# The order of a 27,000-instruction program is chosen among several hundred plans, and the first chunk's y gets tiles of its own

## Chip, core and metric

One core of a Trainium2 chip. The metric is the device time of one execution in microseconds, the median of several runs. The kernel is timed on one core; nothing is shared with the others.

## The reference

An RWKV-7 attention block, then a feed-forward block with SiLU. Everything is float32 on the chip.

```python
# r, k, v, w, a, b: (batch 4, heads 8, seq 768, head_dim 40)
for t in range(S):
    y[:, :, t] = np.einsum('bhd,bhde->bhe', rt, state)
    Sa = np.einsum('bhde,bhe->bhd', state, at)
    state_decay = state * wt[:, :, None, :] - np.einsum('bhd,bhe->bhde', Sa, bt)
    state = state_decay + np.einsum('bhd,bhe->bhde', vt, kt)
...
x = y.transpose(0, 2, 1, 3).reshape(3072, 320)
h = x @ w_in                      # (320, 2048)
g = h * (1.0 / (1.0 + np.exp(-h)))
out = g @ w_out                   # (2048, 320)
```

w_in and w_out come in as float64 and are turned into float32 on the chip.

## The kernel before

The sequence is cut into 12 chunks of 64 steps. Within a chunk the recurrence is solved in closed form: products of decays by scans on VectorE (DVE), products of a with b and k (`between`), the inverse of a unit triangular 64x64 matrix for each of the 32 pairs of batch and head, then u = X R (`solve`, `solve_t`), y from u, v and the state (`look`, `write`, `write_state`, `scaled`), and the new state (`update`). Each chunk's y, 256 tokens by 320, goes through the feed-forward block (`moe`): `full` and `rest` are x @ w_in, `gate` is Silu on ScalarE, `second` (L1319) is g @ w_out.

The functions, with the lines where their instructions are recorded:

- `load` (L449, L459) and `load_r` (L476, L485): inputs of a chunk, on SP's DMA queue. `prepare(n)`: scans (`down` L509 to L511, `between_`, `up` L529), kb (`aside` L548) and a (`scale` L538) on DVE, `between` (L566), `masked` (L613), `sv` (L628), R's copy (L640), `turn` (L653) and its copies to kt (L666).
- `special(n)`, chunks 0 to 2: the inverse from 16-blocks. The blocks go through memory (ms L583, xs L755), `dots` on DVE (L679, L680), back through zs (L765) to mi (L771), then `both` (L797), `turn` (L810) and three `more` (L842), each with an addition on DVE (L857).
- `inverse(k)` and `merge(n)`, chunks 3 to 11: two chunks at a time, 32-blocks by `dots` on DVE, out through zd (L879) and, after a copy on ScalarE (L885), xd (L886), and back (L897, L909); `merge` joins halves with two TensorE operations, `first` (L923) and `second` (L952).
- `chain(n)`: `right` (L995), `total` (L1005), `solve` (L1019), `solve_t` (L1050), a transpose of the state (L1080, copy L1093), `update` (L1107) and two additions to the state (L1123).
- `read(n)`: two `look` (L1149), masked on DVE (L1161), `write_state` (L1185), `write` (L1200), `scaled` (L1211). Chunk 0 does `write` and `scaled` in two halves and sends y straight to the x tile `xt` by twelve transfers, six on SP and six on ScalarE (L1254); the others send it through memory (L1229, then `bring`, L1269, L1271).
- `moe(n)`: `full` (L1281), `rest` (L1294), `gate` (L1304), `second` (L1321), copy (L1333), output (L1336).
- `weights(n)`: ten pieces of the weights, each 1 MB as float64, fetched by GpSimd (L363) into space that is otherwise used later (the g tile, parts of wo, a raw tile, the XI tile), and converted by DVE and ScalarE (L368 to L386); three pieces use TensorE for a sum (`sum_`, L392).

All of these only record operations. `Plan.add` notes engine, estimated cost, what is read and written, a priority `pri`, and the `Room`s that the operation needs: a room is one of four PSUM tile pairs (`pair`) or one of two SBUF tiles (`lam`), which it holds until its last operation. `Plan.order` (L100) makes one list of all operations: at each step it takes, for every engine, the ready operation with the least estimated start plus `URGE[engine] * pri`, and of these the earliest. For TensorE the estimate counts instruction blocks and half speed before 42 us (`walk`). The list is emitted as it is, so each engine works through its own part in that order, and a semaphore wait at its head holds back all that is behind it. What goes to SP's, ScalarE's and GpSimd's DMA queues stands in the same list.

In `read(0)` the two `look` results and y take `lam` rooms, of which there are two; chunk 1's `masked` takes the same kind:

```python
pl, la = Room("pair", 2), Room("lam", 3)
...
py_, yx = {part: Room("pair", 3 if n else 2) for part in parts}, Room("lam", 1)
```

Of the kernel before, what the change touches and what calls it, by code (L numbers as in the profile page):

```python
# [3 lines left out]

# [26 lines left out]


class Plan:

# [65 lines left out]
    def order(self):  # L100
        ops = self.ops
        self.fetched, self.count, self.shape = [0.0, 0.0], 0, "Q"
        nexts = [[] for _ in ops]
        for op in ops:
            op["wait"] = len(op["before"])
            for b in op["before"]:
                nexts[b].append(op)
        ready = {e: [op for op in ops if op["engine"] == e and not op["wait"]] for e in self.HOP}
        at = dict.fromkeys(self.HOP, 0.0)
        out, held = [], {}  # L110
        queue = dict.fromkeys(("SP", "ACT", "POOL"), 0.0)
        for op in ops:
            op["ready"] = 0.0
        while len(out) < len(ops):
            best = None
            for e, some in ready.items():
                starts = []
                for op in some:
                    s = max(at[e], op["ready"])
                    for room in op["rooms"]:  # L120
                        if room.slot is None:
                            free = self.free[room.kind]
                            fits = free and held.get((room.kind, room.most), 0) < room.most
# [45 lines left out]
            out.append(op)  # L169
        return out  # L170

@with_exitstack
def kernel(
    ctx: ExitStack,
# [17 lines left out]
    D, H, P, Q = 40, 8, 4, 16  # L192
# [35 lines left out]
    at = ring("a", 3, Q * C)  # L228
# [29 lines left out]
    def vec(n):  # L258
        return 0.15 + n * 0.00104
# [871 lines left out]
    def read(n):  # L1131
# [7 lines left out]
        lam = []  # L1139
        for m in range(2):  # L1140
            pl, la = Room("pair", 2), Room("lam", 3)
# [14 lines left out]

            add("PE", 0.9, look, rk + vtk + [("ut", m)], [pl], pri, [pl, la], 128)
            add(
                "DVE",
                vec(1024),  # L1160
                lambda pl=pl, la=la: nc.vector.tensor_tensor(  # L1161
                    out=la.tile.rearrange("p (q t) -> p q t", q=Q),
                    in0=pl.tile.rearrange("p a b -> p (a b)").rearrange("p (q t) -> p q t", q=Q),
                    in1=ml.unsqueeze(1).to_broadcast([128, Q, C]),
                    op=ALU.mult,
                ),
                [pl],
                [la],
                pri,
                [pl, la],  # L1170
            )
# [46 lines left out]
        for part in parts:  # L1218
            used = [lam[m] for m in part]
            if n:  # L1220
                add("PE", 0.9, partial(write_state, py_[part]), [*rk, "GT"], [py_[part]], pri, [py_[part]], 128)
            add("PE", 0.87 * len(part), partial(write, part, py_[part]), ktk + used, [py_[part]], pri, [py_[part], *used], 64 * len(part), shape="H")
            add("DVE", vec(512 * len(part)), partial(scaled, part, py_[part]), [py_[part], *allw], [yx if len(part) == 2 else (yx, part)], pri, [py_[part], yx] if part is parts[0] else [py_[part]])
        yxk = [yx] if len(parts) == 1 else [(yx, part) for part in parts]
        if n >= ND:
            yx.left = 3
            for j in range(2):
                dma(
                    lambda j=j: nc.sync.dma_start(  # L1229
                        xh[n].rearrange("(p j e) t -> j e p t", p=P, j=2)[j],  # L1230
                        yx.tile[rows(j)].rearrange("e (p t) -> e p t", p=P),
                    ),
                    160,
                    yxk,
                    [("xh", n, j)],
                    pri,
                    rooms=[yx],
                )
            return
        pieces_ = []  # L1240
# [8 lines left out]
        for i, (h, r0, r1, d) in enumerate(pieces_):  # L1249
            k = r0 // 128  # L1250
            e = "ACT" if n == 0 and i % 2 else "SP"
            p0, s0 = d.start + r0 - 128 * k, 64 * (h % 2) + r0 - D * h
            dma(
                lambda h=h, k=k, e=e, p0=p0, s0=s0, m=r1 - r0: (nc.scalar if e == "ACT" else nc.sync).dma_start(  # L1254
                    xt[p0 : p0 + m, k], yx.tile[s0 : s0 + m, h // 2 * T : h // 2 * T + T]
                ),
                (r1 - r0) * 1.0,
                yxk,
                [("xt", k + (k == 2 and d.start > 0), h)],
                pri,  # L1260
                e,
                [yx],
            )

    def bring(n):
# [270 lines left out]
```

## Time and profile before

| | us |
|---|---|
| median of 3 runs | 747.25 |
| lowest, highest | 745.65, 751.07 |
| profiled execution, its own time | 744.45 |
| profiled execution, first to last instruction (span) | 742.7 |
| TensorE busy | 673.2 |
| VectorE busy | 418.7 |
| ScalarE busy | 193.7 |
| first TensorE matmul starts | 13.34 |
| first `full` of chunk 0 starts | 74.55 |
| first `full` of chunk 1 starts | 154.58 |
| last `second` ends | 735.0 |

Times in the profile count from the first instruction. PE is TensorE, PEld its weight loads, DVE VectorE, ACT ScalarE, POOL GpSimd, SPq and ACTq the queues by which SP and ScalarE issue transfers. A wait names the engine and the line that ended last before it; "issue" is time in which nothing that the profile records was missing. The slices on the page are 18.6 us each; a digit is a share in tenths. PEclk is the clock that TensorE was granted. A float32 matmul shows as two records, so an operation of 32 matmuls has x64.

### The profile page before, as it was taken

What the parts mean: (1) busy time and instruction counts of PE and PEld (TensorE: products, weight loads), DVE (VectorE), ACT (ScalarE), POOL (GpSimd) and SP (SyncE); (2) the same over time, 40 slices, a digit from 0 to 9 for tenths busy, and PEclk for the clock granted to TensorE, in tenths of its full rate; (3) what the DMA queues carried; (4) which work ended last, traced back from release to release, by engine and by line L of the source; (5) the groups of instructions that cost most, each with busy time, mean ns of one, the idle gap of its engine ahead of it and who ended that gap; (6) DMA issues with size and microseconds to landing.
All of it is one profiled execution on the core that took longest, in us unless ns stands there. A gap on an engine that the chain in (4) does not pass through costs nothing.

```text
span 742.7 us, 27297 instructions
## 1 busy us (share of the span) xinstructions
PE 673.2 (91%) x12666; PEld 541.9 (73%) x12666; DVE 418.7 (56%) x614; ACT 193.7 (26%) x241; POOL 16.8 (2%) x31
## 2 busy tenths in 40 slices
PE   2177989999899999999699999999998999999995
PEld 2175668678778788877578878878877778778774
DVE  6847679797479345388228595372694576111000
ACT  3252626423303313104211405222115112102020
POOL 3300000000000000000000000000000000000000
PEclk9999999899999999999899999999997999999999
DMA  7670665722731554514334706443315213201001
GB/s 246 157 224 25 185 211 172 212 67 59 173 98 54 122 145 120 155 25 98 80 95 125 200 9 153 109 124 101 92 36 113 82 38 94 62 16 41 18 1 22
DMA packets 117979, 77.15 MB, mean 104 GB/s; under 512 B 65506, under 2 KB 114338, under 8 KB 117218
## 3 DMA queue, kind: packets, MB, share of 16 engines
q1 hardware_dynamic: 113352, 64.54, 33.3%
q0 software_dynamic: 2096, 10.49, 4.3%
q8 instruction: 101, 1.65, 0.9%
q10 hardware_dynamic: 2410, 0.30, 0.3%
q14 instruction: 20, 0.16, 0.1%
HBM read 60.29 MB, written 14.61 MB: 101 GB/s over the span
## 4 chain that ended last, share of the span: by engine, by line
PE 77%; DVE 8%; issue 5%; DMA 3%; SPq 2%; ACT 2%; ACTq 0%; DVEq 0%
PE pair L1321 27%; PE pair L1281 19%; PE pair L1294 5%; PE pair L1149 3%; PE pair L1200 3%; PE pair L566 3%; PE pair L842 2%; PE pair L1107 2%; PE pair L1019 2%; PE pair L628 2%; PE pair L1050 2%; PE pair L392 2%; PE pair L952 2%; PE pair L995 1%; PE pair L1185 1%
## 5 line engine op out<-in xcount | busy, mean ns | idle before, releaser
L1321 PE MATMUL pair<-wo,gts 128*128 128x320 f32 x768 | 219.6, 442 | 1.5 <-issue 1.5
L1321 PEld LDWEIGHTS pair<-wo,gts 128*128 128x128 f32 x768 | 145.1, 193 | 60.8 <-issue 5.0
L1281 PE MATMUL pair<-xt,wi 128*128 128x256 f32 x768 | 177.9, 390 | 3.4 <-DMA xt<-lam 3.4
L1281 PEld LDWEIGHTS pair<-xt,wi 128*128 128x128 f32 x768 | 147.3, 195 | 26.6 <-issue 4.5
L1304 ACT ACTIVATE gts<-pair 128x1024 f32<-128x1024 f32 x48 | 46.5, 1020 | 120.4 <-PE pair L1294 113.2
L1333 DVE COPY ot<-pair 128x320 f32<-128x320 f32 x24 | 11.7, 488 | 88.2 <-PE pair L1321 87.1
L680 DVE TENSOR_REDUCE XI<-XI 128x64 f32<-128x512 f32 (+9 forms) x85 | 58.6, 690 | 2.9
L566 PE MATMUL pair<-a,kb 40*64 40x64 f32 x1536 | 31.4, 233 | 30.1 <-issue 16.0
L566 PEld LDWEIGHTS pair<-a,kb 40*64 40x64 f32 x1536 | 27.8, 145 | 32.6 <-issue 30.7
L1161 DVE TENSOR_TENSOR lam<-pair,ml 128x1024 f32<-128x1024 f32 x24 | 29.1, 1222 | 37.0 <-PE pair L1149 37.0
L1294 PE MATMUL pair<-xt,wi 64*128 64x256 f32 x384 | 48.0, 389 | 0.0
L1294 PEld LDWEIGHTS pair<-xt,wi 64*128 64x128 f32 x384 | 35.2, 187 | 6.3 <-issue 2.0
L1211 DVE TENSOR_TENSOR lam<-pair,wz 128x1024 f32<-128x1024 f32 (+1 forms) x13 | 14.8, 1142 | 38.5 <-PE pair L1200 38.4
L679 DVE TENSOR_TENSOR XI<-XI,mi 128x1024 f32<-128x1024 f32 (+8 forms) x60 | 33.6, 560 | 3.0 <-DMA mi<-md 1.6
L640 ACT COPY R<-pair 128x640 f32<-128x640 f32 x12 | 8.3, 692 | 98.4 <-PE pair L628 98.3
L548 DVE TENSOR_TENSOR kb<-kbv 128x512 f32<-128x512 f32 (+1 forms) x36 | 29.9, 859 | 0.4
L1149 PEld LDWEIGHTS pair<-r,vut 40*64 40x64 f32 x1536 | 24.8, 135 | 6.1 <-issue 4.5
L1149 PE MATMUL pair<-r,vut 40*64 40x64 f32 x1536 | 27.8, 221 | 0.4 <-issue 0.4
L511 DVE TENSOR_TENSOR_SCAN kbv<-wz,zt 128x1024 f32<-128x1024 f32 x12 | 27.5, 2291 | 0.6
L529 DVE TENSOR_TENSOR_SCAN wz<-wz,zt 128x1024 f32<-128x1024 f32 x12 | 27.5, 2290 | 0.3
L1200 PEld LDWEIGHTS pair<-lam,kt 128*40 128x40 f32 x768 | 22.1, 117 | 5.8 <-issue 3.3
L885 ACT COPY mi<-XI 128x1024 f32<-128x1024 f32 x5 | 10.1, 2015 | 62.3 <-DVE XI L680 62.3
(144 smaller groups left out, 690.7 us busy)
## 6 DMA issues: line engine op xcount, KB each, us to landing
wz<-in_wT SPq DMA_DIRECT2D x12, 512.0 KB
kbv<-in_bT SPq DMA_DIRECT2D x12, 512.0 KB
a<-in_aT SPq DMA_DIRECT2D x12, 512.0 KB
kbv<-in_kT SPq DMA_DIRECT2D x12, 512.0 KB
r<-in_rT SPq DMA_DIRECT2D x48, 96.0 KB
vut<-in_vT SPq DMA_DIRECT2D x48, 96.0 KB
vu<-in_v SPq DMA_DIRECT2D x24, 160.0 KB
out<-ot SPq DMA_DIRECT2D x48, 80.0 KB
```

What stands on the lines that cost most here:

```text
L511: nc.vector.tensor_tensor_scan(back(V), back(W[:, 2 : 2 + Q * C]), zt, 1.0, ALU.mult, ALU.add)
L548: TTn[engine].tensor_tensor(out=at_(kb, place(is_b, first), (576 * step, 4 // step), (128, 4), (1, C)), in0=blocks((kf, bf)[is_b]), in1=bl ...
L566: nc.tensor.matmul(room.tile[half(b), j, g * C : g * C + C], lhsT=kb[rows(j), place(is_b, q) : place(is_b, q) + C], rhs=A[rows(j), q * C : ...
L679: nc.vector.tensor_tensor(out=at_(tmp, 0, *dims), in0=x, in1=y, op=ALU.mult)
L680: nc.vector.tensor_reduce(out=out_, in_=at_(tmp, 0, *dims), axis=AX.X, op=ALU.add)
L1149: nc.tensor.matmul(pl.tile[half(1 - b if role else b), b, c * C : c * C + C], lhsT=vut[rows(b), role, hu, :], rhs=rs[rows(b), hh, :], star ...
L1161: lambda pl=pl, la=la: nc.vector.tensor_tensor(out=la.tile.rearrange("p (q t) -> p q t", q=Q), in0=pl.tile.rearrange("p a b -> p (a b)").r ...
L1200: nc.tensor.matmul(py.tile[rows(j), b, c * C : c * C + C], lhsT=K[:, q, j], rhs=lam[m].tile[:, l * C : l * C + C], start=fresh(py, b, j), ...
L1281: nc.tensor.matmul(rooms[g].tile[:, f // 2, (f % 2) * T : (f % 2) * T + T], lhsT=wi[:, k, (4 * g + f) * 128 : (4 * g + f) * 128 + 128], rh ...
L1294: nc.tensor.matmul(rooms[g].tile[:, h, (f % 2) * T : (f % 2) * T + T], lhsT=wi3[half(h), g * 256 + (f % 2) * 128 : g * 256 + (f % 2) * 128 ...
L1304: nc.scalar.activation(out=gts[:, 4 * g * T : 4 * g * T + 4 * T], in_=rooms[g].tile.rearrange("p a b -> p (a b)"), func=AF.Silu)
L1321: nc.tensor.matmul(po[b].tile[:, 0, 0:DM], lhsT=g4[:, f, 128 * b : 128 * b + 128], rhs=wo[:, f, :], start=f == 0, stop=f == NF - 1,)
```

## The change

The plan isn't ordered once but 410 times, and the list is kept that takes least in a model of the run. `best(10, 400)` first orders with the settings as they are, then nine times with random `URGE` and `COLD`; then, 400 times, it takes a random group of operations of the best list (same engine, cost and priority), shifts their priority by 1, 2, 4 or 8 up or down, orders again, and keeps the list if it is no worse. The random numbers have a fixed seed, so the program is always the same. The model, `through`, walks a finished list with costs as estimated, and adds up three passes: as they are; with slower DMA and a longer wait for an instruction block when DMA is busy; and with that, longer hops between engines and a slower DVE. TensorE is at half speed in it in each stretch of 3.41 us that follows one with under 0.42 of work.

Besides, chunk 0's two `look` results and its y no longer take `lam` rooms. They go to the tiles `at[0]` and `sbs[0]`, and to `Xs[0]`, which chunk 0 has used by then; the keys of these tiles are added to what the operations write and read, so that they wait for the earlier readers. All operations and their instructions are as before; their order, and which tile of a kind they get, differ.

```diff
     def order(self):
...
-                    room.tile = self.slots[room.kind][room.slot]
...
+    SLOW = 2.8, 1.7
+    CASES = (1.0, 300.0, 0.15, 1.0), (1.5, 240.0, 0.15, 1.0), (1.5, 240.0, 0.25, 1.04)
+    WINDOW, FEW = 3.41, 0.42
+
+    def through(self, out, crowd, rate, hop, slower):
...
+                    if len(fetched) == block + 1:
+                        full = crowd if max(queue.values()) > t + 1 else 0.0
+                        fetched.append(max(t + 0.4, fetched[-1] + before) + after + full)
+                    if count >= gate:
+                        t = max(t, fetched[-1] + 0.1)
...
+                        w = int(t / width)
+                        pace = 0.5 if t > 30 and work.get(w - 1, 0.0) < few * width else 1.0
...
+        return max(end)
+
+    def best(self, draws, steps):
...
+            spans = [self.through(out, *case) for case in self.CASES]
+            return sum(spans), out, {i: room.slot for i, room in rooms.items()}
...
+                moved = dict(best[1][2])
+                by = rng.choice((-8, -4, -2, -1, 1, 2, 4, 8))
+                for n in rng.choice(groups):
+                    moved[n] = moved.get(n, 0.0) + by
+                setting = *best[1][:2], moved
+            got = value(*setting)
+            if best is None or got[0] <= best[0][0]:
+                best = got, setting
...
@@ def read(n):
+            if n == 0:
+                la.tile, lk = ((at[0], [("a", 0)]), (sbs[0], [("sb", 0)]))[m]
+                lks += lk
+            lr = [la] if n else []
...
-            add("PE", 0.9, look, rk + vtk + [("ut", m)], [pl], pri, [pl, la], 128)
+            add("PE", 0.9, look, rk + vtk + [("ut", m)], [pl], pri, [pl, *lr], 128)
...
+        if n == 0:
+            yx.tile = Xs[0]
+        yr, yk = ([yx], []) if n else ([], [("X2", 0, 0), ("X2", 0, 1)])
...
-        for op in plan.order():
+        for op in plan.best(10, 400):
             op["do"]()
```

More of the change, by code (lines that the diff above doesn't have):

```diff
@@ L3 @@
 from math import prod
+from random import Random
 import concourse.bass as bass
@@ L169, in order @@
             out.append(op)
+        return out
+    SLOW = 2.8, 1.7
+    CASES = (1.0, 300.0, 0.15, 1.0), (1.5, 240.0, 0.15, 1.0), (1.5, 240.0, 0.25, 1.04)
+    WINDOW, FEW = 3.41, 0.42
+    def through(self, out, crowd, rate, hop, slower):
+        at = dict.fromkeys(self.HOP, 0.0)
+        queue = dict.fromkeys(("SP", "ACT", "POOL"), 0.0)
+        end, free = [0.0] * len(out), {}
+        fetched, count, shape, work = [0.0, 0.0], 0, "Q", {}
+        before, after = self.SLOW
+        width, few = self.WINDOW, self.FEW
+        for op in out:
+            e = op["engine"]
+            s = at[e]
+            for b in op["before"]:
+                s = max(s, end[b] + (hop if self.ops[b]["engine"] != e else 0.0))
+            for place in op["takes"]:
+                s = max(s, free.get(place, 0.0))
+            if e == "PE":
+                self.shape = shape
+                t, shape = s + self.turn(op), op["shape"]
+                to_ = count + op["k"]
+                step = op["cost"] / op["k"]
+                while count < to_:
+                    block = count // 256
+                    gate = 256 * block + 194
+                    if len(fetched) == block + 1:
[3 more added lines that the diff above has]
+                        t = max(t, fetched[-1] + 0.1)
+                    to = min(to_, gate if count < gate else 256 * block + 256)
+                    left, count = (to - count) * step, to
+                    while left > 1e-9:
+                        w = int(t / width)
+                        pace = 0.5 if t > 30 and work.get(w - 1, 0.0) < few * width else 1.0
+                        d = min((w + 1) * width - t + 1e-9, left / pace)
+                        work[w] = work.get(w, 0.0) + d
+                        t += d
+                        left -= d * pace
+            else:
+                t = s + op["cost"] * (slower if e == "DVE" else 1.0)
+            at[e] = t
+            if op["size"]:
+                begin, work_ = max(queue[e], t), op["size"] / rate
+                both = max(0.0, max(queue[o] for o in queue if o != e) - begin)
+                queue[e] = begin + (2 * work_ if work_ < both / 2 else work_ + both / 2)
+                for o in queue:
+                    if o != e and queue[o] > begin:
+                        queue[o] += min(work_, both / 2)
+                t = queue[e] + self.LAND
+            end[op["n"]] = t
+            for place in op["gives"]:
+                free[place] = max(free.get(place, 0.0), t + 0.1)
+        return max(end)
@@ new lines, in best, with value @@
+    def best(self, draws, steps):
+        rng = Random(1)
+        rooms = {id(room): room for op in self.ops for room in op["rooms"]}
+        steps_of = {i: room.left for i, room in rooms.items()}
+        first = [op["pri"] for op in self.ops]
+        groups = {}
+        for op in self.ops:
+            groups.setdefault((op["engine"], round(op["cost"], 2), round(op["pri"], 1)), []).append(op["n"])
+        groups = list(groups.values())
+        def value(urge, cold, moved):
+            self.URGE, self.COLD = urge, cold
+            self.free = {k: [(0.0, i) for i in range(len(v))] for k, v in self.slots.items()}
+            for i, room in rooms.items():
+                room.slot, room.left = None, steps_of[i]
+            for op in self.ops:
+                op["pri"] = first[op["n"]] + moved.get(op["n"], 0.0)
+                op["takes"], op["gives"] = [], []
+            try:
+                out = self.order()
+            except AssertionError:
+                return 1e9, None, None
+            seen = set()
+            for op in out:
+                for room in op["rooms"]:
+                    place = room.kind, room.slot
+                    if id(room) not in seen:
+                        seen.add(id(room))
+                        op["takes"].append(place)
+                    op["gives"].append(place)
+            spans = [self.through(out, *case) for case in self.CASES]
+            return sum(spans), out, {i: room.slot for i, room in rooms.items()}
+        best = None
+        for i in range(draws + steps):
+            if i < draws:
+                urge = dict(self.URGE)
+                if i:
+                    urge = {**urge, "PE": rng.uniform(0.03, 0.1), "DVE": rng.uniform(0.06, 0.14), "ACT": rng.uniform(0.02, 0.05)}
+                setting = urge, rng.choice((24.0, 42.0)) if i else self.COLD, {}
+            else:
+                moved = dict(best[1][2])
[6 more added lines that the diff above has]
+                best = got, setting
+        (_, out, slots), _ = best
+        for i, room in rooms.items():
+            if room.slot is not None or slots[i] is not None:
+                room.slot = slots[i]
+                room.tile = self.slots[room.kind][room.slot]
@@ L1138, in read @@
         rk, vtk = [("r", b, j) for b in range(2) for j in range(2)], [("vt", b, j) for b in range(2) for j in range(2)]
-        lam = []
+        lam, lks = [], []
         for m in range(2):
-            pl, la = Room("pair", 2), Room("lam", 3)
+            pl, la, lk = Room("pair", 2), Room("lam", 3), []
             lam.append(la)
+            if n == 0:
+                la.tile, lk = ((at[0], [("a", 0)]), (sbs[0], [("sb", 0)]))[m]
+                lks += lk
+            lr = [la] if n else []
             def look(m=m, pl=pl):
@@ L1167, in read @@
                 [pl],
-                [la],
+                [la, *lk],
                 pri,
-                [pl, la],
+                [pl, *lr],
             )
@@ L1221, in read @@
                 add("PE", 0.9, partial(write_state, py_[part]), [*rk, "GT"], [py_[part]], pri, [py_[part]], 128)
-            add("PE", 0.87 * len(part), partial(write, part, py_[part]), ktk + used, [py_[part]], pri, [py_[part], *used], 64 * len(part), shape="H")
-            add("DVE", vec(512 * len(part)), partial(scaled, part, py_[part]), [py_[part], *allw], [yx if len(part) == 2 else (yx, part)], pri, [py_[part], yx] if part is parts[0] else [py_[part]])
+            add("PE", 0.87 * len(part), partial(write, part, py_[part]), ktk + used + lks, [py_[part]], pri, [py_[part], *(used if n else [])], 64 * len(part), shape="H")
+            add("DVE", vec(512 * len(part)), partial(scaled, part, py_[part]), [py_[part], *allw], [yx if len(part) == 2 else (yx, part), *yk], pri, [py_[part], *(yr if part is parts[0] else [])])
         yxk = [yx] if len(parts) == 1 else [(yx, part) for part in parts]
+        yxk += yk
         if n >= ND:
@@ L1236, in read @@
                     pri,
-                    rooms=[yx],
+                    rooms=yr,
                 )
@@ L1261, in read @@
                 e,
-                [yx],
+                yr,
             )
```

## The prediction

> **What bounds the kernel now.** I read the page first (busy times, slices), then TensorE's waits, then the timeline of TensorE and ScalarE, and last the table of stretches. The page:
>
> ```profile
> PE 673.2 (91%) x12666; PEld 541.9 (73%) x12666; DVE 418.7 (56%) x614; ACT 193.7 (26%) x241; POOL 16.8 (2%) x31
> PE   2177989999899999999699999999998999999995
> PEclk9999999899999999999899999999997999999999
> ```
>
> TensorE is the bound: slices of 9 from the fourth on, no other engine near it. But busy isn't full speed. I took for each planned operation the duration it has in the timeline at full clock (a `full` 3.55 us, half of the 7.10 of a pair; a `rest` 1.93; a `second` of the output product 2.18, one eighth of 17.42; a 64-matmul group 1.0 to 1.1, `write` 1.92, `update` 1.36, one step of `more` 2.0) and multiplied by its count: 48 x 3.55 + 24 x 1.93 + 96 x 2.18 = 426 us for the feed-forward part, and about 225 us for all small operations. That is 650 us, the same before and after, since no operation is added or removed. The last output product ends at 735 us. So 85 us are lost; they are what a new order can win. Where, from the timeline: 41 us before 71.1 (30 us of work is done by then), 16 between there and 154.6 (97.5 us done), 26 from 154.6 to the end.
>
> TensorE's longest waits:
>
> ```profile
> PE pair L566 <- issue: 16.0, 4, 13.9
> PE pair L566 <- DVE a L538: 14.0, 2, 13.3
> PE pair L1019 <- issue: 3.9, 2, 3.0
> PE pair L1281 <- DMA xt<-lam: 3.4, 1, 3.4
> PE pair L1107 <- issue: 2.9, 1, 2.9
> PE pair L952 <- ACT sb L291: 1.5, 1, 1.5
> ```
>
> The columns are total, times, longest. The two of 13 to 14 us are the start (DVE prepares chunk 0, then solves the 16-blocks of chunk 0). The rest are single holes. The timeline shows them, and what they do to the work behind them:
>
> ```profile
> 74.55 5.38 PE L1281 MATMUL pair<-xt,wi 128*128 128x256 f32 x16 [3.38 <-DMA xt<-lam]
> ...
> 104.07 0.35 PE L1107 MATMUL pair<-vu,kt 128*40 128x40 f32 x6 [2.94 <-issue]
> 104.35 5.41 PE L1281 MATMUL pair<-xt,wi 128*128 128x256 f32 x16
> ...
> 361.03 1.39 PE L1019 MATMUL pair<-R,X 64*64 64x40 f32 x41 [3.04 <-issue]
> 362.35 3.57 PE L1321 MATMUL pair<-wo,gts 128*128 128x320 f32 x8
> ```
>
> A `full` is 3.72 us in this view, but 5.4 after a hole of 3 us; a `second` 3.57 instead of 2.42. The waits on "issue" fall in the middle of an operation (58 of 64 matmuls, a hole, then 6), so no data is late: the instructions are. ScalarE shows one more thing:
>
> ```profile
> 70.92 5.03 ACTq L1254 DMA_DIRECT2D xt<-lam  x6
> 76.08 1.14 ACT L372 ACTIVATE gts<-gts 128x1024 f32<-128x1024 int32 x1 [7.28 <-DVE wi L368]
> ```
>
> While it issues six transfers of chunk 0's y it does nothing else for 5 us.
>
> **What the Trainium skill says.** "TensorE: Matmul & The Clock Gate", Part 1, says the array's clock is halved after an idle window of about 3.4 us and comes back after about as long a busy one. The trace agrees: the stretch 75 to 80 us has a mean granted clock of 0.70, 104 to 110 0.72, 362 to 366 0.66. "Runtime: NRT & Kernel Launch", section Instruction fetch mechanics, says an engine fetches blocks of 256 instructions by a DMA queue of its own, and that crossing a block is mostly hidden. The trace has such a queue (instruction, 101 packets), but here it isn't all hidden: the "issue" waits after 154 us sum to about 12 us. They stand where several 64-matmul groups follow each other (128 instructions, loads included, in 1.1 us) or DMA is busy (0.83 in 80 to 104 us). "ScalarE: Activation LUTs", What ACT_TABLE_LOAD costs, gives 1283 ns for a table switch; the trace has 1.28 us at 110.90, ahead of the first Silu.
>
> **The change, part by part.** The order is read from the two built programs.
>
> *Own tiles for chunk 0.* With `at[0]`, `sbs[0]` and `Xs[0]` chunk 0's two `look` no longer share the two `lam` tiles with chunk 1's `masked`. TensorE now has look, look, two sums, write, write, solve, where before six operations (`sv` among them) stood between the two writes. No instruction is added. A new wait is: `scaled` writes Xs[0], so it waits for `solve` and `solve_t` to have read X. By rows: looks 57.4 to 59.4, sums to 61.4, writes to 63.4, solve to 64.4, `scaled` twice 0.69 on DVE to 66.0 (before: 70.9). The transfer took 3.6 us from there, so xt is there at 69.6 instead of 74.5. What is late next: ScalarE's R copy now stands behind the six transfer issues (66 to 71.1), and `full` takes the pair tile that copy frees, so `full` starts at 71.9, not 69.6. It saves 2.6 us of wait and, if the clock holds, 1.7 of half speed: 4.3 by its end.
>
> *Loads moved on SP's queue.* Chunk 1's eight r and v^T loads (5.0 us of SP at 80.0) and one 512 KB load of chunk 4 now go ahead of the eight mi transfers of chunk 1's special. `write_state` (needs r) comes forward, and with it three sums instead of one. By the same rows mi is issued from 75.3 to 79.3 and lands at about 82 (81.4 before); by then TensorE has 3 us more behind it. Of that 1.6 us goes back, since `both` and `turn` now take the same pair tile and wait for ScalarE's copy. Net at the end of `more` about 0.7.
>
> *95 to 110 us.* Before, write_state, solve, solve_t, update stand in a row (512 instructions in 4.5 us), then comes the 2.94 us hole and a half-speed `full`. Now they alternate with `full` (3.55) and `rest` (1.93): hole and half speed go, 2.94 + 1.7 + 0.6 of waiting for the u copy. A new wait of 1.4 comes: solve_t takes the pair tile that the first Silu frees, behind the table switch. Gain at that point 4.4.
>
> *110 to 155 us.* DVE gets the first output weights earlier, since POOL's fetch for tile A is no longer queued behind the one that needs XI (POOL waited 20.5 us for L842). 1 us is lost where `between` waits for the Silu of `rest`. The waits and half clock at 131 to 139 us (1.5 + 1.0 + 2.3; clock 0.57 in that stretch) go, since right stands behind sv and the weights are done. I get 148 instead of 154.6 by adding rows; I take 5 to 6 of these 6.6.
>
> *After 155 us.* The same 26 us of holes: 5.8 at 353 to 366 (0.9, 3.0 of fetch, 1.2 half speed), 6.6 at 562 to 579 (X from the inverse late, then half clock), the rest single ones under 1.5. In the new order the merges (`first`, `second`) stand between the `full`s, so their copies are covered; between chunk 10's `between` and chunk 9's `first` there are 50.3 us of TensorE work instead of 45.2, and 2.6 us less DVE work stands ahead of the inverse's end. Fully removed that is 12; but I count 10 blocks of 256 instructions with under 2.8 us of work in each order, so as many chances for a fetch hole. I take 3 + 3 less 1 for new holes: 5.
>
> *First 57 us.* Operations stand in the same places, save chunk 0's two turns behind the second `between` and one DVE product earlier. Both hide under the 13.9 us hole, where DVE works without a pause: 0. If the cover fails, at most the 1.2 us of the product.
>
> Sum: -6 - 5 = -11. Span 742.7 - 11 = 731.7; around it lie 744.45 - 742.7 = 1.75, so 733.5 for an execution like the profiled one, which is 2.8 under the median of 747.25. Predicted median 736.
>
> Bounds of what the trace doesn't show: early part 2 (clock not kept, mi 3 us late) to 8; late part -1 (each removed hole comes back as another) to 14. Together 1 to 22 us of gain; I take 11.
>
> **Rivals.**
> (a) Only the start is won: 741 to 745, middle 743. The later holes are of fetch and of the free-running clock window, and a new order moves them. For it: equally many dense blocks. Against: the two largest have a named cause that is now covered.
> (b) Nearly all named holes go: 16 to 20 us, 729. Against: the single waits on fetch depend on DMA traffic that no order fixes.
> (c) Slower: mi<-zs of chunk 1 lands late. Place: SP, behind nine loads. When the queues were full, at 40 us, eight transfers of that shape took 13.0 us of SP instead of 4 to 5. Then mi lands near 90 instead of 82; TensorE idles 8 us, runs `both` and `turn` at half clock (1.7), and everything behind waits, as the weights' XI tile comes free after special. That is 8 + 1.7 - 3 brought forward = +6.7, and with no gain later 754. It decides if the transfers take over 9 us. Against it: DMA was 0.15 busy in 60 to 80 us.
> That the change doesn't do what it says is out: the orders differ in all queues.
>
> **Numbers.** Forecast 0.52, (a) 0.26, (b) 0.13, (c) 0.09. A measurement of this kernel can tell about 1% (7.5 us) from no change. Faster by more needs under 739.8: nearly all of the forecast's share and all of (b), 0.61; within 1%: 0.31; slower: 0.08. Range 725 to 748: it takes (b) and (a), and leaves (c) out.
>
> **What would show it.** Right: no wait of 3 us on xt, clock 1.0 in 70 to 80 us; chunk 1's first `full` near 148 to 149 us; no "issue" wait over 2 us after 90 us; TensorE's lost time after that point 21 us or less. Wrong: mi<-zs waits of several us at 80 us; "issue" waits after 154 us near 12 us in all again; first `full` of chunk 1 at 153 or later.

## The result, and the profile after

| us | before | after |
|---|---|---|
| median | 746.1 (6 runs, 744.55 to 751.07) | 738.03 (6 runs, 735.14 to 742.53) |
| ratio | | 0.9894, 95% interval 0.985 to 0.9938 |
| profiled execution, its span | 744.45, 742.7 | 742.53, 740.8 |
| last `second` ends | 735.0 | 732.83 |

The gain is 8.1 us; the forecast was 11, to 736. A second series of the unaltered changed kernel, run with the experiments below, gave 740.46 against 743.71 (ratio 0.9893, 0.9836 to 0.9951). In that series and in two of the experiments the executions lie so far apart (here 729.9 to 743.9) that the ratio leaves out the longest of them (three of six in the last); the medians given are over all, and by them the second series' gain is 3.3 us. By the ratios both series show 8 us, with intervals that reach from 4 to 12.

One warning ahead of any reading: the profiled execution of after is the longest of its six, and that of before, 744.45, is shorter than any of the six of before. The traces differ by 1.9 us of span, the medians by 8.1. A trace shows here where time is won and lost; it doesn't show the whole sum.

The page of after, for the three lines that the prediction showed of before:

```profile
PE 674.7 (91%) x12666; PEld 540.5 (73%) x12666; DVE 419.5 (57%) x614; ACT 194.6 (26%) x241; POOL 14.3 (2%) x31
PE   2179799898899999999999999899999999999995
PEclk9996999999999999999999999999998999999998
```

Busy time is the same, as it must be. New is the 6 in the fourth slice of the clock: TensorE is at half speed there. Then the longest waits of TensorE (total, times, longest):

```profile
PE pair L682 <- DVE a L654: 28.7, 2, 14.9
PE pair L682 <- issue: 5.5, 6, 2.8
PE pair L1166 <- issue: 3.2, 2, 2.8
PE pair L1223 <- DVE vu L411: 2.1, 3, 0.8
PE pair L1166 <- ACT gts L1428: 1.6, 1, 1.6
PE pair L1405 <- ACT R L756: 1.3, 1, 1.3
```

Lines have moved: L1405 is `full`, L1166 `solve_t`, L682 `between`, L1445 `second`. The wait of 3.4 us on xt is gone, as are the two of 3 us at `update` and `solve`. In their place stand two waits on issue of 2.8, at other operations. The timeline tells where:

```profile
53.04 0.26 PE L1166 MATMUL pair<-X,R 64*40 64x64 f32 x3 [2.76 <-issue]
...
77.24 5.33 PE L1405 MATMUL pair<-xt,wi 128*128 128x256 f32 x16 [1.32 <-ACT R L756]
...
102.06 3.72 PE L1405 MATMUL pair<-xt,wi 128*128 128x256 f32 x16
...
111.76 1.10 PE L1166 MATMUL pair<-X,R 64*40 64x64 f32 x64 [1.62 <-ACT gts L1428]
...
198.79 0.69 PE L682 MATMUL pair<-a,kb 40*64 40x64 f32 x31 [2.77 <-issue]
199.41 14.88 PE L1445 MATMUL pair<-wo,gts 128*128 128x320 f32 x48
```

At 102 us things are as forecast: a `full` at full clock (3.72, before 5.41), and behind it 1.6 us of wait on the first Silu's pair tile (1.4 was forecast). At 53 and 199 us stands what wasn't forecast.

To compare stages I add up what TensorE lost in each: its idle time, and busy time times one minus the granted clock, from stretches of 3 us. The end less this sum is 658.4 us for before and 659.4 for after, so the account closes to 1 us.

| lost, us | to first `look` | to chunk 0's first `full` | to chunk 1's first `full` | to 350 | 350 to 580 | to the end | sum |
|---|---|---|---|---|---|---|---|
| before | 34.2 | 4.8 | 12.0 | 6.2 | 17.7 | 1.7 | 76.6 |
| after | 35.2 | 6.2 | 8.3 | 13.2 | 9.2 | 1.3 | 73.4 |
| after, second profile | 35.6 | 6.2 | 10.5 | 13.1 | 7.8 | 3.1 | 76.3 |

The largest two changes are seen without arithmetic in the table of stretches (length, TensorE busy, clock, DMA share, GB/s), first of before, then of after:

```profile
154.58:350.00 195.42, 189.26 (x3596) 1.00 0.39 100
350.00:580.00 230.00, 218.90 (x4614) 0.96 0.41 103
```

```profile
153.99:350.00 196.01, 186.29 (x3623) 0.98 0.39 102
350.00:580.00 230.00, 224.05 (x4582) 0.99 0.38 99
```

Between 350 and 580 us, 8.5 us are won (9.9 in the second profile); between 154 and 350, 7 are given back, in both profiles, and both have the hole at 199 to 200 us (2.77 and 2.42). So it is no single chance, it goes with the order.

### The profile page after: what moved, and what is told of

Same layout as the page of the kernel before. It is cut to its first block, busy times and chain, and to the rows that moved or that the text cites. A ratio compares the mean times of both kernels' runs of the same rounds, so it can differ in the third digit from the quotient of the medians.

```text
span 740.8 us, 27279 instructions
## 1 busy us (share of the span) xinstructions
PE 674.7 (91%) x12666; PEld 540.5 (73%) x12666; DVE 419.5 (57%) x614; ACT 194.6 (26%) x241; POOL 14.3 (2%) x31
## 4 chain that ended last, share of the span: by engine, by line
PE 80%; DVE 8%; DMA 3%; ACT 3%; issue 3%; SPq 1%; ACTq 1%; DVEq 0%
PE pair L1445 27%; PE pair L1405 21%; PE pair L1418 5%; PE pair L1269 4%; PE pair L682 3%; PE pair L1323 3%; PE pair L958 2%; PE pair L1135 2%; PE pair L1223 2%; PE pair L1068 1%; PE pair L1166 1%; PE pair L508 1%; PE pair L744 1%; PE pair L1308 1%; PE pair L1111 1%
## 5 line engine op out<-in xcount | busy, mean ns | idle before, releaser
L1445 PE MATMUL pair<-wo,gts 128*128 128x320 f32 x768 | 219.8, 442 | 1.1 <-issue 1.1
L1445 PEld LDWEIGHTS pair<-wo,gts 128*128 128x128 f32 x768 | 144.7, 192 | 60.4 <-issue 4.3
L1405 PE MATMUL pair<-xt,wi 128*128 128x256 f32 x768 | 175.5, 386 | 1.6 <-ACT R L756 1.3
L1405 PEld LDWEIGHTS pair<-xt,wi 128*128 128x128 f32 x768 | 145.7, 192 | 24.5 <-ACT R L756 1.4
L682 PE MATMUL pair<-a,kb 40*64 40x64 f32 x1536 | 32.2, 236 | 35.8 <-DVE a L654 28.7
L682 PEld LDWEIGHTS pair<-a,kb 40*64 40x64 f32 x1536 | 28.6, 149 | 38.5 <-issue 20.5
L1281 DVE TENSOR_TENSOR lam<-pair,ml 128x1024 f32<-128x1024 f32 x22 | 26.4, 1220 | 32.9 <-PE pair L1269 30.4
L1334 DVE TENSOR_TENSOR lam<-pair,wz 128x1024 f32<-128x1024 f32 x11 | 13.5, 1223 | 38.8 <-PE pair L1323 38.8
L795 DVE TENSOR_TENSOR XI<-XI,xs 128x1024 f32<-128x1024 f32 (+1 forms) x25 | 25.3, 1010 | 0.8
L407 ACT ACTIVATE vu<-pair 64x640 f32<-64x640 f32 x13 | 9.1, 698 | 60.3 <-PE pair L1135 59.4
```

Source lines behind the costliest of these rows:

```text
L682: nc.tensor.matmul(room.tile[half(b), j, g * C : g * C + C], lhsT=kb[rows(j), place(is_b, q) : place(is_b, q) + C], rhs=A[rows(j), q * C : ...
L795: nc.vector.tensor_tensor(out=at_(tmp, 0, *dims), in0=x, in1=y, op=ALU.mult)
L1281: lambda pl=pl, la=la: nc.vector.tensor_tensor(out=la.tile.rearrange("p (q t) -> p q t", q=Q), in0=pl.tile.rearrange("p a b -> p (a b)").r ...
L1405: nc.tensor.matmul(rooms[g].tile[:, f // 2, (f % 2) * T : (f % 2) * T + T], lhsT=wi[:, k, (4 * g + f) * 128 : (4 * g + f) * 128 + 128], rh ...
L1445: nc.tensor.matmul(po[b].tile[:, 0, 0:DM], lhsT=g4[:, f, 128 * b : 128 * b + 128], rhs=wo[:, f, :], start=f == 0, stop=f == NF - 1,)
```

## The experiments

My theory going in: each part of the change is worth part of the gain (T), and the search wins because its model puts the borders of TensorE's instruction blocks where there is work to cover the fetch (F). Rivals: one part does all; or borders don't matter and covered data waits are the gain (G). "The planner's figure" is the mean of `through`'s three passes; it is what the planner believes, no time of the chip.

**1. The parts alone, and the fetch term.** All four on one chip, before 743.71.

Tiles alone, ordered by the settings as they are (`order` sets the rooms' tiles again):

```diff
-        for op in plan.best(10, 400):
+        for op in plan.order():
```

> Chunk 0's own tiles, with the planner's single old order in place of the search. Theory T (each part is worth part of the 8 us, and the search pays mainly behind 80 us): the start becomes shorter, xt is there before 72 us instead of 74.5, the holes behind 155 us remain; 741 to 744 us. Rival S (the tiles do nothing by themselves, the search does all): 746 +- 2. Rival W (an order with the tiles that was not searched meets worse holes): over 748. The planner's own mean figure falls by 5.6 us (742.8 to 737.2).

Measured: 739.6, ratio 0.9946 (0.9923 to 0.9969), 4 us faster, a little better than T's range. With TensorE at full clock the start goes as the prediction's step has it:

```profile
73.89 3.72 PE L1406 MATMUL pair<-xt,wi 128*128 128x256 f32 x16 [1.44 <-ACT R L757]
```

`full` waits for ScalarE's copy behind the transfer issues, not for xt, and runs at full clock. From the first `look` to it there are 15.48 us (forecast 14.5, before 17.17).

The search alone, tiles shared as before:

```diff
-            if n == 0:
+            if False:
                 la.tile, lk = ((at[0], [("a", 0)]), (sbs[0], [("sb", 0)]))[m]
```

(and likewise for y)

> The search alone; chunk 0's y shares its tiles as before. Theory T: 740 to 743, the 3.4 us wait on xt stays. Rival S: 738, as with both parts. Rival N (the search only moves holes about and the tiles do all): 745 to 747. The planner's own figure falls by 13.7 us (742.8 to 729.1).

Measured: 736.14, ratio 0.9901 (0.9862 to 0.9939): rival S. The search alone brings all that both bring, with 6.2 us of idle time between the first `look` and chunk 0's `full`. Most of that is one wait for a copy of u that stands behind ScalarE's six transfer issues (66.3 to 71.3 us):

```profile
72.14 0.36 PE L1223 MATMUL pair<-vu,kt 128*40 128x40 f32 x4 [4.49 <-ACT vu L407]
```

The tiles are worth 4 us with the old order and nothing that can be seen with a searched one.

The changed kernel unaltered:

> The changed kernel unaltered, on the chip of the other three, for its time beside theirs and for a second profile. If the 2.8 us hole at 53 us and the half clock from 53 to 66 us are a chance of one execution, this profile lacks them or has them elsewhere, its looks start near 57.4 and its span is 733 to 738; if the new order has them always, they are here again and the span is near 740.

Measured: 740.46, profiled at 743.94. The hole is there again, at 53.6 us (1.81), and half speed behind it. Both profiled executions are the longest of their series, so this shows that the order can have it, not how often it has.

The search without the fetch wait in `through` (the fetch estimate in `order` stays):

```diff
-                    if count >= gate:
-                        t = max(t, fetched[-1] + 0.1)
```

> The search with the fetch term of its model left out (the wait at instruction 194 of each block of 256); own tiles kept. By the full model this order is 734.1, against 725.1 for the changed kernel and 737.2 for the tiles with the old order. Theory F (the fetch term describes the chip): about 4 to 5 us slower than the changed kernel, 742 to 743, with more wait on issue behind 155 us. Rival G (holes fall where DMA traffic happens to be, and the term buys nothing): within 2 us of the changed kernel.

Measured: 743.68, ratio 0.9999 (0.9973 to 1.0025). That is what F expects: without that term 410 orders are worth nothing, and even what the tiles bring is lost. Its trace, longest waits of TensorE:

```profile
PE pair L680 <- DVE a L652: 28.6, 2, 15.0
PE pair L680 <- issue: 5.2, 6, 1.2
PE pair L1306 <- issue: 4.0, 3, 2.0
PE pair L956 <- issue: 3.9, 2, 2.0
PE pair L1164 <- issue: 3.1, 3, 1.5
```

The data waits behind 60 us are fewer than in after (10.7 against 15.7 us), those on issue more (16.0 against 10.3; before 15.3). This search, which doesn't see the fetch, traded one for the other.

**2. Moving the borders and nothing else.** If borders decide, then useless products on TensorE, in the 13 us in which it has nothing to do, must change the time while no operation is moved:

```diff
+        idle = 32
         for op in plan.best(10, 400):
+            if op["engine"] == "PE":
+                for _ in range(idle):
+                    nc.tensor.matmul(pairs[3][:, 1, 448:512], lhsT=ident, rhs=ident[:, 0:64], start=True, stop=True)
+                idle = 0
             op["do"]()
```

> The changed kernel with 32 useless 128x64 products on TensorE ahead of its first operation (64 instructions), where it is idle for 13 us: no work is added on the path, but every border of 256 instructions falls 64 instructions earlier in the work. Theory F (the order pays since it puts the fetch borders where there is work to cover them): the gain is lost, 745 to 752; the planner's figure for this order goes from 725.1 to 750.7, and the waits on issue behind 60 us rise from about 10 to over 15. Rival G (the order pays by covered waits on data, borders don't matter): 736 to 740, waits on issue as in the changed kernel.

> The kernel before, its order untouched, with 104 useless 128x64 products (208 instructions) in the same idle time. Theory F: 3 to 5 us faster than before, by the borders alone; the planner's figure goes from 742.8 to 738.1. Rival G: within 1 us of before.

> The kernel before with 48 useless products (96 instructions) in the same idle time. Theory F: clearly slower, by 10 to 30 us; the planner's figure goes from 742.8 to 774.6. Rival G: within 1 us of before.

With them, on one chip (before 745.81), more search: `plan.best(10, 3000)`.

> The changed kernel with 3000 moves in the search in place of 400. The planner's figure goes from 725.1 to 718.2. Theory M (the figure and the chip go together at about half the size, as 17.7 became 8): 3 to 4 us faster than the changed kernel, 734 to 735 where that has 738. Rival O (400 moves have found what is real, further moves fit the model's own errors): within 1 us of the changed kernel, or slower.

The three with products were built badly. A float32 product is four instructions, not two, and this form isn't cheap: of the first kernel,

```profile
L1509 PE MATMUL pair<-ident x64: 420/421/448, 6.5 to 19.9; 128*128 128x64 f32 x64
```

two records each, one every 0.21 us. They ended at 20.3, 27.1 and 51.0 us, so the first operation came 6.5, 13.8 and 37.7 us late, and the borders moved by 128, 192 and 416 instructions. Measured: 737.69, 765.31 and 786.32 (ratios 0.9894, 1.025, 1.0529). The last two slow down by 19.5 and 40.5: their late start and 3 to 6 us more. They decide nothing of what they were made for. (The edit is shown for the changed kernel; the other two have it in the kernel before, with 104 and 48.) The first is worth a look: with a start 6.5 us late it is as fast as the changed kernel, where the planner's figure for a shift of 128 is 739.5 against 725.1, 14 us worse. The figure is wrong about borders, and the traces say how.

**Where the borders are.** A trace has TensorE's instructions one by one, so the place of each wait on issue in its block of 256 can be counted. Counted in matmuls and weight loads alone the place creeps, while the planner puts it at 194 throughout. But TensorE's queue also holds wait instructions of its own; under `look` of after, for instance:

```profile
L1269 PEldq EVENT_SEMAPHORE  x16: 51/51/51, 56.0 to 660.2; - x16
```

There are 107 of them in before and 107 in after. Counted with the rest, from the first weight load on, they leave one place:

| | wait ends, us | block | place in matmuls and loads | wait instructions ahead | place |
|---|---|---|---|---|---|
| before | 43.09 | 2 | 183 | 9 | 192 |
| before | 104.07 | 13 | 165 | 28 | 193 |
| before | 361.03 | 49 | 127 | 66 | 193 |
| before | 614.40 | 89 | 93 | 99 | 192 |
| after | 53.04 | 4 | 181 | 12 | 193 |
| after | 198.79 | 27 | 147 | 46 | 193 |
| after | 464.48 | 65 | 115 | 78 | 193 |

Of the 194 waits on issue in the fourteen traces 183 stand at 192 or 193. Of the others, five are the long wait of 13.5 to 15.3 us near the start, five are waits of 0.16 us at one `sv`, and one is 0.44 us.

What they wait for is in the traces too. The page of before has a queue of instruction fetches (packets, MB, share):

```profile
q8 instruction: 101, 1.65, 0.9%
```

These are packets of 16 KB, about one for each block. Each of the 183 waits ends 1.2 to 1.6 us after its block's packet has landed (the 13th for block 13): the one at 104.07 after a packet that started at 101.89 and landed at 102.86, the one at 361.03 after 358.51 and 359.39. From block 1 on, TensorE passes place 192 in no block of any trace sooner than 1.19 us after that landing. So these waits are waits for the fetch.

The planner misses two things: the wait instructions, and 24 instructions of the twelve `sum_`, for which it takes two each where the trace has four. Together its borders are off by 52 instructions at 104 us and by 131 at the end. (The expectations below speak of 118 wait instructions by block 89; the trace has 99 there, and these 24.)

More search is 735.6, ratio 0.9871 (0.9831 to 0.9911), between its theories: its figure fell 6.9 us further, its ratio is 0.2% under the changed kernel's, which is too little to tell the two apart (0.9831 to 0.9911 and 0.985 to 0.9938).

**3. Cheap products, and a search with the true borders.** One chip, before 744.42. The products now are 64 wide with 40 rows, ended by 10.7 us, and nothing starts later; borders move by 128.

```diff
-                    nc.tensor.matmul(pairs[3][:, 1, 448:512], lhsT=ident, rhs=ident[:, 0:64], start=True, stop=True)
+                    nc.tensor.matmul(pairs[0][0:64, 1, 0:64], lhsT=ident[64:104, 0:64], rhs=ident[64:104, 0:64], start=True, stop=True)
```

> The changed kernel with 32 useless 64x64 products (64 matmul records and 64 loads, 128 instructions) on TensorE ahead of its first operation, some 2 us in its idle first 13 us, so that nothing starts later and only the borders of 256 instructions move, by half a block. Theory C (the waits on issue stand at one fixed place of each 256 instructions, and the planner's figure puts it wrongly, by more and more along the list, since it leaves the separate wait instructions of TensorE's queue out, 118 by block 89): 5 to 9 us faster than the changed kernel, near 731, with 5 us or less of waits on issue behind 60 us. Theory F as the planner's figure has it: 14 us slower (725.1 to 739.5), near 752. Rival G (borders don't matter): as the changed kernel.

Measured: 735.28, ratio 0.9873 (0.983 to 0.9916). The waits on issue behind 60 us fell to 4.7 us, as C expects, but the gain over the changed kernel's ratio is 1.5 us, not 5 to 9, and the intervals overlap: by its time this is rival G. The waits on data behind 60 us rose from 15.7 to 18.6 us. The planner's +14 is refuted.

> The kernel before, its order untouched, with the same 32 useless products. Theory C: faster by 6 to 10 us (corrected borders give 720.8 in place of 730.7), so near 737, as much as the whole change brought; the wait of 3 us at 104 and the one at 361 us are gone or under 1 us. Theory F as the planner's figure has it: 24 us slower (742.8 to 767.1). Rival G: as before.

Measured: 747.75, ratio 1.0047 (1.0016 to 1.0078), 3.5 us slower. All theories miss; C has the wrong sign. The wait at 361 us is gone, as C expects. The one at 104 us isn't, and there is a new one:

```profile
104.35 0.45 PE L1050 MATMUL pair<-X,R 64*40 64x64 f32 x7 [3.90 <-issue]
104.72 2.37 PE L1107 MATMUL pair<-vu,kt 128*40 128x40 f32 x64
...
135.70 0.70 PE L566 MATMUL pair<-a,kb 40*64 40x64 f32 x16 [2.23 <-issue]
```

With the borders half a block earlier, the hole at 104 us falls into `solve_t` in place of `update`, at the same time. Four operations of 128 instructions stand in a row there: wherever borders fall, a run of 512 holds two. This shift didn't help there, while the searched order, which breaks up the run at 95 to 110 us, has no hole in it. Why the median is 3.5 us slower the trace doesn't show: its waits on issue behind 60 us are 11.7 us, those of before 15.3, and the profiled execution (743.15) is the second shortest of 13. The 13 have a mean granted clock of 0.968, those of before on this chip 0.974.

Then the search itself with the borders where the traces have them (its formula comes within 11 instructions of them), with own tiles and the cheap products:

```diff
-    SLOW = 2.8, 1.7
+    SLOW = 2.4, 1.1
...
+    FIRST, GATE = 128, 186
+
+    def border(self, b):
+        return 256 * b - min(3.2 * b, 38 + 0.9 * b)
...
-                    gate = 256 * block + 194
+                    gate = self.border(block) + self.GATE
```

> The same 32 useless products, own tiles, and the search (400 moves) with its border put where the traces have it: a border every 256 instructions less min(3.2 b, 38 + 0.9 b) for the wait instructions up to block b, the first one half a block early, the wait 186 instructions into the block, and the fetch times fitted to the waits of seven traces (2.4 and 1.1 us in place of 2.8 and 1.7). Its figure falls from 715.1 (the changed order with the products) to 709.5. Theory C: 2 to 5 us faster than the changed order with the products, 727 to 730. Rival D (with the borders out of the way the search has nothing left to gain): as that one, within 1 us.

Measured: 728.91, ratio 0.9784 (0.9746 to 0.9821): 15.5 us faster than before, 6.4 faster than the changed order with the same products on the same chip, and at the time that C expects. Its stretches:

```profile
153.08:350.00 196.92, 190.41 (x3791) 1.00 0.41 107
350.00:580.00 230.00, 226.70 (x4572) 1.00 0.38 100
```

From 153 us on it loses 10.6 us (after: 23.7) and is at full clock all the way; waits on issue behind 60 us are 3.2 us. Three things differ from the search before it, though: the places, the fetch times, and `FIRST`, by which the search knows of the half block that the products take. The last run takes the places back and leaves the other two:

```diff
-    FIRST, GATE = 128, 186
+    FIRST, GATE = 128, 194
...
-        return 256 * b - min(3.2 * b, 38 + 0.9 * b)
+        return 256 * b
```

> As the run with the corrected search, with one thing taken back: the borders stand again at every 256 planned instructions and the wait at 194, so they drift off the true ones along the list; the 32 useless products, the smaller fetch times (2.4 and 1.1 us), the moves and the seed stay. Theory P (the true places made the 6 us between the two orders with the products): 734 to 736, the waits on issue behind 60 us back at 5 to 10 us. Theory Q (the smaller fetch times did, since a search that overrates the fetch spends its moves on it): 728 to 730, as the corrected one; the corrected figure gives this order 710.5, that one 709.5 and the changed order with the products 715.1.

Measured, on another chip (before 744.78): 731.83 over all six, which is 0.983 of before. That lies between P and Q, with 6.9 us of waits on issue (P: 5 to 10). But its executions run from 722.2 to 735.5, and its ratio, taken as in the section on the result, is 0.9731 (0.9663 to 0.9799), which is Q. So it isn't shown that the true places add anything. What the smaller fetch times and `FIRST` bring together is clear by the ratios (0.9731 against 0.9873 of the changed order with the products) and small by the medians (0.983 against 0.987); no run parts the two. The trace fits Q's reason: waits on data behind 60 us are 8.9 us instead of 18.6, those on issue 6.9 instead of 4.7. The two last orders are the fastest here.

What this comes to: that the single holes are waits for the fetch is shown by the packets, and that a searched order alone brings the gain is shown by the run without the tiles. The search needs its fetch term (0.9999 without it), but F as I posed it is out, since the gain stays when every border moves by half a block. A rival that no run tests is that the term works as a charge on dense runs, wherever it puts the borders. And each searched order is one draw from one seed; no second seed was run, so a few us between two of them can be of the draw.

## Why the prediction was right, and where it wasn't

The time is that of the forecast, and its main cause held: the waits in dense runs of small products can be won by order. But the sum of 6 + 5 came out by other terms. Of the five signs that I named for being right, the profiled execution has one, no wait on xt. The clock isn't 1.0 from 70 to 80 us (half speed from 77.1 to 80.5), chunk 1's first `full` is at 153.99, a wait on issue after 90 us is 2.77, and TensorE loses 23.7 us after 154. So the traces don't carry the number, and that it came so close is in part luck.

Three readings were off, without weight for the forecast. The slices of 9 begin with the fifth, not the fourth (7). And the three parts of the loss add up to 83 us, not 85, where the account above has 76.6: it leaves the slow first 40 us (`between` takes 1.99 us there, 1.16 later) in the 658, as the clock's record begins behind them. Last, 1283 ns is what "ScalarE: Activation LUTs", What ACT_TABLE_LOAD costs, gives for the table load alone; a whole switch is about 2.66 us there, of which the trace shows the load's 1.28.

- *Own tiles, 4.3 us.* The mechanism is right: tiles alone gave 4 us, with the wait moved to ScalarE's copy behind six issues. In after:

```profile
70.79 5.66 ACTq L1378 DMA_DIRECT2D xt<-X  x6
76.49 0.69 ACT L756 COPY R<-pair 128x640 f32<-128x640 f32 x1 [5.44 <-DMA xt<-X]
```

But all of it is 5 us late in after: the transfers were to be issued at 66. The condition "if the clock holds" failed.
- *First 57 us, 0.* This is the step that failed. I looked for what the moved turns hide under, and not for what they do to the borders behind them. In the changed order the fetch wait falls into `solve_t` at 53.04 (2.76; before had 2.35 at 43.1 and 1.62 at 50.2, both ahead of it), and TensorE drops to half speed until 66.9. The looks take 3.69 us, where each took 1.16 in before, four sums 3.78 instead of 2.06. Chunk 0's first `full` starts at 77.24, forecast 71.9, before 74.55. To that point after has lost 41.4 us, before 39.0. The 5.3 us by which that `full` is later than forecast stay in what follows.
- *SP's queue, mi at 82.* It landed in time, though some 5 us later than forecast like all else: TensorE waited 0.43 us for it at 87.8. The rival (c) is out.
- *95 to 110 us, 4.4.* Right: no hole, no half-speed `full`, and the new wait of 1.62 at its place.
- *110 to 155, 5 to 6.* Right, from where it starts. The figures 4.3, 0.7, 4.4 and 5 to 6 are gains reached by a point (otherwise they don't sum to 6), so from chunk 0's first `full` to chunk 1's the forecast is 76 to 77 us (71.9 to 148 or 149). Before took 80.0, after 76.8 (78.2 in the second profile); the lost time there fell from 12.0 to 8.3 us. Chunk 1's first `full` is at 153.99, 5 to 6 us later than forecast, because chunk 0's is. With the tiles alone, where chunk 0's starts at 73.89, it is at 149.02.
- *After 155, 5.* The two stretches that I named at 353 and 562 us gave more than the 6 taken, 8.5 between 350 and 580. The "less 1 for new holes" was 7: the hole at 198.79, half speed behind it, and smaller ones. I had counted as many chances for a fetch hole in both orders and then priced them at 1. So the late part is half wrong.

In the profiled executions the losses fall by 3.2 us (and by 0.3); the medians fall by 8.1 and 3.3. The other executions of after have a mean granted clock of 0.978 to 0.985 where the profiled one has 0.976. Over all its 12 executions span and clock go together (correlation -0.82); over 65 executions of before the mean clock is 0.974, over these 12 it is 0.980, and 0.0065 of 743 is 4.8 us, of a difference of 6.2 in mean span (742.9 and 736.7). That fits a gain of which a good part is half speed that doesn't set in, but it compares means, and no run shows it. Which of the holes set it off in an execution without a trace stays open. Open too is why the tiles' 4 us vanish in the searched order: the half speed at 53 to 66 us would do it, but no run took that hole away alone. And a start 6.5 us late cost only some 1.6 us in the end (0.9894 against 0.9873 for the cheap products); the trace has 5 us less lost between 150 and 350 us, and I don't know why.

## What to carry to other kernels

When an engine's waits end on "issue" inside an operation, write down their places in that engine's instruction stream modulo the block before believing any story; if they agree, look whether a packet of instructions lands just ahead of each. A planner that places such waits must count every instruction of the queue, the wait instructions too. Break up long runs of very short instructions; shifting one didn't help here. A planner is worth what its terms are worth: without the fetch term 410 orders gave nothing, with it 3 to 8 of 17.7 us promised (742.8 to 725.1), and with fetch times fitted to traces, and the products known to the search, 13 to 16 by the medians.

## What the runs showed of the hardware

- The Trainium skill, "Runtime: NRT & Kernel Launch", section Instruction fetch mechanics, says that blocks of 256 instructions are fetched while others run, so that the fetch is mostly hidden. Here it isn't in dense stretches: waits of up to 3.9 us, at place 192 or 193 of a block, which end 1.2 to 1.6 us after the block's packet has landed.
- "TensorE: Matmul & The Clock Gate", Part 1, says that full clock returns after about one busy window of 3.4 us. After the hole at 361 us in before it was so (0.50 to 364.4, then 0.96), with `second`. After 53 us in after it took 13.7 us (53.2 to 66.9) of TensorE without a gap, of which this is a part:

```profile
53.04:64.20 11.16, 11.16 (x250) 0.51 0.06 16
```

In it stand products of 40 and 64 rows, and sums of 128x512. The second profile and the two last runs show 10.3 to 13.7 us at the same place. Small size alone doesn't explain it: behind the hole at 43.1 in before, products of 40 and 64 rows had full clock again after 3.4 us (43.9 to 47.3). Why it took longer here stays open.
- 32 products with 128x128 weights and 64 columns took 13.9 us when nothing but themselves was in the queue, 32 with 40x64 weights 7.05: 434 and 220 ns each, both in the slow first 40 us. Filler isn't free by being useless; the first form made the start late.
